# Attention scores from 64x32 tiles, value products from 64x64 and 32x64 tiles, in a fused attention and mixing kernel

## The chip, the cores and the metric

One NeuronCore of a Trainium2 chip. The metric is device microseconds (us) of one execution. The names of engines: PE is TensorE (matmul), PEld its weight loads, DVE VectorE, ACT ScalarE, POOL GpSimd, SP the engine whose queue issues nearly all DMA transfers. "Stationary" is the operand of a matmul that is loaded into the array, "moving" the one that streams through it. A tile "RxC" is a part of PE's array with R rows (the contraction) and C columns (the stationary operand's columns, which become output partitions).

## The reference

Eight batches, eight heads, 576 positions, 64 columns a head. Two parts: attention in a narrow window, then a mixing block on its result.

```python
B, H, S, D = q.shape                      # 8, 8, 576, 64
scores = (1 / sqrt(D)) * q @ k^T
rel = pos[:, None] - pos[None, :]
mask_plain = (rel >= 0) & (rel < 32)                       # heads 0 to 3
mask_dil = (rel >= 0) & (rel < 128) & (rel % 4 == 0)       # heads 4 to 7
attn = softmax(where(mask, scores, -1e9))
x = concat_heads(attn @ v)                # [B, 576, 512]

theta = x @ w_theta                       # 512 x 512
zr, zi = x * cos(theta), x * sin(theta)
y = w_tok_r @ zr + w_tok_i @ zi           # over positions, 576 x 576
u = x + y
out = u + relu(u @ w_ch)
```

All is f32. The host reorders the positions of the dilated heads so that every fourth position stands together: then they too have a window of 32, inside four segments of 144.

## The kernel before

Heads go in pairs, four pairs a batch (heads 2p and 2p+1 are pair p; NP is 4). A pair's 576 queries are 18 blocks of 32 (QB), and a block sees 64 keys (BW): its own 32 and the 32 ahead of them.

- `scores` (matmuls at line 614): per block one f32 matmul with 128 rows (64 columns of one head over 64 of the other) and 64 columns: the query tile is block-diagonal, the host has put zeros where a head meets the other head's rows. Block 2n goes to output partitions 0 to 63 and block 2n+1 to 64 to 127, so 18 matmuls on two column tiles fill nine groups of 64 keys: five groups in one PSUM bank of tag `s`, four in the next. The second bank is claimed after the first's matmuls are issued.
- `mask_scores` (line 553, DVE): adds the mask, negates and takes the row's bound, one instruction for each of the nine groups. `exp` on ACT (line 649), row sums and reciprocal on DVE (652, 653), and on POOL the product with the reciprocal (line 655) give the probabilities `P`, 128 partitions x 576: quadrants of 32 partitions are (block parity e, head).
- `turn` (line 673, DVE): eight transposes, 32 partitions x 288 each, write P turned into `pt`, which holds per group and head 128 keys x 64 queries, block-diagonal, with zeros that POOL wrote once. Only batch 0 does this on PE: `flip` multiplies P by an identity into PSUM tiles `pT` (line 709), and DVE and ACT copy them into `pt` (684, 687).
- `pv` (line 773): per group and head one f32 matmul with 128 rows (keys of two blocks, one over the other), 64 value columns and 64 queries: 18 matmuls on two column tiles into `o`. Value tiles come as `va` (five groups) and `vb` (four). `x_evac` (line 733) copies `o` to `x` in SBUF, undoing the order of the dilated heads.

Then come `theta` (tile `th`, line 842), cosine and sine (DVE, ACT, POOL), the token mixing and the channel product (`c`, line 1477). For batches 0 and 1 the token mixing is direct (`y`, line 1444, eight units of 24 or so matmuls each), from batch 2 (FIRST) on it is a fast scheme that multiplies sums of blocks, in steps A, B, C and D (line 1235). These large products use operands split in two parts (names ending in h and l) and the whole array, 128 rows x 128 columns.

What sets the order. The class `Order` runs all these functions as generators. Each says which engine it wants next and for how many ns (`yield "PE", 1060`) or which event it waits for (`yield None, ("pt", b, pr)`), and `Order` lays the instructions of each engine out in one fixed sequence by rank and these numbers, before the program is built. On the chip each engine follows its sequence and waits on semaphores. For the start (batches 0 and 1) a table RANK sets ranks; from batch 1's token mixing on, `phase(b)` writes a plan: eight or more token steps of batch b, between them the scores and value products of batch b+1 (or b+2), then theta of b+1 and the channel units of b. Each entry has a due time from a cost in us.

Loads of q and k (`load_qk`) and of values are issued on SP's queue two pairs or so ahead. Batch 0 has its own tiles (`first_k`, `first_v`) and `mask_on_pe`, which adds the mask by a bf16 matmul.

Of the kernel before, what the change touches and what calls it, by code (L numbers as in the profile page):

```python
# [20 lines left out]
QB = 32  # L21
BW = 2 * QB
NJ = S // (2 * QB)
VA = 5
NC = DM // 128
# [187 lines left out]
SLACK = 500  # L213
LATENCY = dict(PE=100.0, DVE=100.0, ACT=130.0, POOL=130.0, DMA=1800.0)
# [35 lines left out]
def build(ctx, tc, qT, kT, vw, wth, wtk, wch, maskb, ident, identb, outT):  # L250
# [60 lines left out]
    def load_qk(n):  # L311
        if n >= B * NP:
            return
        b, pr = divmod(n, NP)
        yield "rank", due.get(("scores", b, pr), od.rank)
        r = yield from take("qk", 2)
        if od.steady and b > FIRST and pr < 2:
            yield None, ("vbi", b - 1, pr + 1)
        q = ap.tile([128, 2 * NJ, 2 * QB], F32, tag="q", name=f"q{b}_{pr}")
        k = ap.tile([128, S + 32], F32, tag="k", name=f"k{b}_{pr}")  # L320
        yield "DMA", dma(2 * S)
        pin(nc.sync.dma_start(q, qT[b, pr]))
        yield "DMA", dma(S + 32)
        pin(nc.sync.dma_start(k, kT[b, pr]))
        qks[b, pr] = (q, k, r)
        signal(("qk", b, pr))
# [51 lines left out]
    KE = S + 32  # L378
# [11 lines left out]
    mskb = cp.tile([128, 6, BW], BF16, name="mskb")  # L390
# [5 lines left out]
    def first_loads():  # L396
# [3 lines left out]
        for pr in range(NP):  # L400
# [4 lines left out]
            q = q.rearrange("p a b -> p (a b)").rearrange("p (a b) -> p a b", b=2 * QB)  # L405
            k = first_k[:, KE * pr:KE * pr + KE]
            yield "DMA", dma(2 * S)
# [19 lines left out]
    def consts():  # L427
# [4 lines left out]
        for n in range(2):  # L432
            t = cp.tile([128, NJ, 2, 2 * QB], F32, name=f"pt{n}")
            yield "POOL", 1040
            pin(nc.gpsimd.memset(t, 0.0))
            pts.append(t)
# [99 lines left out]
    def mask_of(pr, j):  # L536
        if j == 0:
            return 1
        return {2: 2, 4: 3, 6: 4, 7: 5}.get(j, 0) if pr >= NP // 2 else 0

    pmats, probs = {}, {}

    def strips():

        for hh in range(2):
            for e in range(2):
                for o in range(2):
                    yield hh, e, o
# [9 lines left out]

    def on_pe(b, pr):
        return b == 0  # L560
# [24 lines left out]
    def scores(b, pr):  # L585
        yield None, ("qk", b, pr)
        if b == 1 and on_pe(b, pr):
            yield None, "sin0"
# [11 lines left out]
        for g0, g1 in ((0, 5), (5, NJ)):  # L600
            ps, rel = yield from bank("s", f"s{b}_{pr}_{g0}")
            ps = ps[:, :(g1 - g0) * BW].rearrange("p (a b) -> p a b", b=BW)
            held[g0] = ps, rel
            if b == 2 and not od.steady:
                yield "LATER", SLACK
            masked = on_pe(b, pr)
            if masked:
                yield "PE", 150
                mask_on_pe(ps, pr, g0, g1)
            yield "PE", (148 if od.steady else 162) * (g1 - g0)  # L610
            for n in range(g0, g1):
                for e in range(2):
                    qb = 2 * n + e
                    pe(nc.tensor.matmul(ps[64 * e:64 * e + 64, n - g0], q[:, qb],  # L614
                                        k[:, QB * qb:QB * qb + BW], start=not masked, stop=not masked or n == g1 - 1))
            if masked:
                go(row_max(b, ps, rel, P, mx, g0, g1, ("mask", b, pr, g0)))
            else:
# [8 lines left out]
        if b and on_pe(b, pr):  # L627
            for g0, (ps, rel) in held.items():
                yield None, ("mask", b, pr, g0)
                yield "EXP", 335 * ps.shape[1]  # L630
                for n in range(ps.shape[1]):
                    table(nc.scalar.activation(P[:, g0 + n], ps[:, n], AF.Exp, bias=mx[:, g0 + n:g0 + n + 1],
                                               scale=SCALE, accum_out=sm[:, g0 + n, :1]))
                give(*rel)
        else:
            for g0 in (0, 5):
                yield None, ("mask", b, pr, g0)
# [5 lines left out]
        elif not on_pe(b, pr):  # L643
# [15 lines left out]
    def turn(b, pr):  # L659
# [4 lines left out]
        yield None, ("pv",) + divmod(b * NP + pr - 2, NP)  # L664
        P, rp = probs.pop((b, pr))
        pmats[b, pr] = pts[pr % 2]
        for i, (hh, e, o) in enumerate(strips()):
            if od.steady:
                yield "TURN" if i < 7 else "DVE", 482
            elif i % 2 == 0:  # L670
                yield "DVE", 940
            k0, p0 = QB * (2 * e + o), QB * (2 * e + hh)
            pin(nc.vector.transpose(pmats[b, pr][k0:k0 + QB, :, hh, QB * e:QB * e + QB],  # L673
                                    P[p0:p0 + QB, :, QB * o:QB * o + QB]))
        give("P", rp)
        signal(("pt", b, pr))

    def flip_evac(b, ps, rel, pr, g0, g1, key):
        for e in range(2):
            es, qs = slice(BW * e, BW * e + BW), slice(QB * e, QB * e + QB)  # L680
            n = (g1 - g0) * BW
            if e == 0:
                yield "DVE", dve(n)
                pin(nc.vector.tensor_copy(pmats[b, pr][es, g0:g1, :, qs], ps[es]))
            else:
                yield "ACT", act(n)
                pin(nc.scalar.copy(pmats[b, pr][es, g0:g1, :, qs], ps[es]))
        give(*rel)
        signal(key)

    def flip(b, pr):

        yield None, ("P", b, pr)
        if pr >= 1:
            yield None, ("fl", b, pr - 1)
        if b or pr >= 2:
            yield None, ("pv",) + divmod(b * NP + pr - 2, NP)
        yield None, "pts"
        pmats[b, pr] = pts[pr % 2]
        P, rp = probs.pop((b, pr))  # L700
        gs = (0, 5), (5, NJ)
        for i, (g0, g1) in enumerate(gs):
            ps, rel = yield from bank(FL0[i] if b == 0 else "xt"[i], f"pT{b}_{pr}_{g0}")
            ps = ps[:, :(g1 - g0) * BW].rearrange("p (a h b) -> p a h b", h=2, b=QB)
            yield "PE", 70 * (g1 - g0)
            for n in range(g0, g1):
                for e in range(2):
                    es = slice(BW * e, BW * e + BW)
                    pe(nc.tensor.matmul(ps[es, n - g0].rearrange("p a b -> p (a b)"), P[es, n], idt[es, es],
                                        start=True, stop=True))  # L710
            go(flip_evac(b, ps, rel, pr, g0, g1, ("fe", b, pr, g0)))
        signal(("fl", b, pr))
        for g0, _ in gs:
            yield None, ("fe", b, pr, g0)
        if b == 0:
            give(f"xh{pr}", 0)
        else:
            give("P", rp)
# [4 lines left out]
    def x_evac(b, pr, ps, rel, key):  # L723
        dst, src = xf[b, pr], ps
        if pr >= NP // 2:
            dst = dst.rearrange("p (j c) -> p c j", c=4)
            src = src.rearrange("p (c j) -> p c j", c=4)
# [29 lines left out]
    def pv(b, pr):  # L757
# [10 lines left out]
        ps = ps_v.tile([128, 2 * DM], F32, tag="v", name=f"o{b}_{pr}")[:, :S]  # L768
        yield "PE", 1060 if od.steady else 1300
        for j in range(NJ):  # L770
            v = va[:, j] if j < VA else vb[:, j - VA]
            for hh in range(2):
                pe(nc.tensor.matmul(ps[64 * hh:64 * hh + 64, BW * j:BW * j + BW], v[:, 64 * hh:64 * hh + 64],  # L773
                                    pmats[b, pr][:, j, hh], start=True, stop=True))
# [962 lines left out]
```

## Time and profile before

| | |
|---|---|
| median of 3 runs | 555.21 us (554.04 to 555.28) |
| profiled execution | 555.45 us, its span 553.7 us |
| PE busy | 528.7 us, 95% of the span, 5296 matmul rows |
| DVE busy | 435.5 us, 79% |
| ACT, POOL busy | 373.1 us (67%), 329.4 us (59%) |
| scores on PE | 1008 + 144 rows |
| value products on PE | 600 + 464 + 72 + 16 rows |
| transposes by `turn` on DVE | 224, 105.1 us |
| moved by DMA | 124.42 MB, mean 225 GB/s |

The span is what the trace covers; the time of an execution has some 1.7 us more around it. A row of the profile reads: line, engine, operation, output tile <- input tiles, shapes, count, then busy us and the mean ns of one, then the idle time of the engine ahead of these instructions and what ended most of it. PE's rows overlap (a matmul's row includes the time until its result is out), so how often one starts tells more than how long it lasts. The windows view gives for each stretch of the span the busy time of each engine, the granted PE clock, the DMA engines' busy share and GB/s. "PE A L1235 x18" in the chain is 18 matmuls of step A in a row on the chain.

### The profile page before, as it was taken

Reading aid. Unit: us, or ns where it says so; the run is one execution under the profiler, and the core shown is the slowest. Engines: PE = TensorE matmul, PEld = TensorE weight load, DVE = VectorE, ACT = ScalarE, POOL = GpSimd, SP = SyncE. Lnnn points to the kernel's source line nnn. Section 1 sums busy time; section 2 is a strip of 40 time slices with the busy share of each in tenths; the row PEclk is TensorE's granted clock in tenths of the full one; section 3 lists DMA queues with packets and bytes.
Section 4 is the critical chain, followed back from the end, with each engine's and each line's share of the span. In section 5 each row is a group of like instructions: output and inputs, shape, how many; then the busy total and the mean of one; then the engine's idle time right before and its main releaser. Section 6 shows DMA issues by size and latency. Waiting matters only on the chain.

```text
span 553.7 us, 14354 instructions
## 1 busy us (share of the span) xinstructions
PE 528.7 (95%) x5296; PEld 478.8 (86%) x5296; DVE 435.5 (79%) x1359; ACT 373.1 (67%) x1029; POOL 329.4 (59%) x347
## 2 busy tenths in 40 slices
PE   5798898999999999999999999999999999999997
PEld 4643887888899899989999899989999899989997
DVE  3878897995588797989799988989799978848322
ACT  1589977858928478768775786768776777467320
POOL 1327868899774175655468375646468365817660
PEclk9999799999999999999999999999999999999999
DMA  8985245633578938994599828993698727680722
GB/s 297 400 332 186 99 139 202 222 144 119 165 256 265 343 155 283 341 282 173 189 326 306 299 86 274 363 281 118 236 325 282 277 90 219 209 274 28 233 85 86
DMA packets 59127, 124.42 MB, mean 225 GB/s; under 512 B 5424, under 2 KB 24624, under 8 KB 58800
## 3 DMA queue, kind: packets, MB, share of 16 engines
q1 hardware_dynamic: 59056, 123.49, 65.1%
q8 instruction: 42, 0.69, 0.5%
q14 instruction: 29, 0.24, 0.1%
HBM read 99.88 MB, written 23.59 MB: 223 GB/s over the span
## 4 chain that ended last, share of the span: by engine, by line
PE 65%; DVE 10%; DMA 9%; ACT 7%; POOL 5%; issue 2%; SPq 1%; POOLq 0%; ACTq 0%; DVEq 0%
PE c L1477 15%; PE th L842 11%; PE C L1235 8%; PE A L1235 7%; PE D L1235 6%; PE o L773 5%; PE B L1235 4%; PE s L614 4%; DVE pt L673 4%; DMA va<-in_vw_dram 3%; PE y L1444 2%; PE th L824 2%; DMA xn<-xd 1%; DMA st_wtk<-in_wtk_dram 1%; DMA q<-in_qT_dram 1%
## 5 line engine op out<-in xcount | busy, mean ns | idle before, releaser
L673 DVE STREAM_TRANSPOSE pt<-P 32x288 f32<-32x288 f32 x224 | 105.1, 469 | 13.1 <-POOL P L655 8.8
L1477 PE MATMUL c<-u,late_wc 128*128 128x288 f32 x768 | 109.1, 296 | 1.2 <-DVE x L1453 1.0
L1477 PEld LDWEIGHTS c<-u,late_wc 128*128 128x128 f32 x768 | 105.5, 188 | 4.7 <-DVE x L1453 1.5
L649 ACT ACTIVATE P<-P,mx 128x64 f32<-128x64 f32 x252 | 84.4, 337 | 2.9 <-DVE mx L553 2.6
L842 PE MATMUL th<-wthh,xh 128*128 128x512 f32 x224 | 75.0, 395 | 0.2 <-DVE K L1377 0.2
L655 POOL TENSOR_TENSOR P<-P,mx 128x576 f32<-128x576 f32 x32 | 38.2, 1192 | 57.6 <-DVE mx L653 50.4
L553 DVE CUSTOM_DVE_ANT_0 P<-s,mskb 128x64 f32<-128x64 f32 x252 | 39.0, 218 | 18.0 <-PE s L614 17.7
L1251 ACT CAST u<-x 128x288 fp32r<-128x288 f32 x48 | 20.6, 430 | 45.3 <-DVE x L1261 44.8
L842 PEld LDWEIGHTS th<-wthh,xh 128*128 128x128 f32 x224 | 42.0, 188 | 9.6 <-DVE K L1377 0.4
L1253 POOL TENSOR_TENSOR u<-x,u 128x288 fp32r<-128x288 f32 x48 | 41.6, 872 | 14.4 <-ACT u L1251 14.0
L649 ACT ACTIVATION_READ_ACCUMULATOR P<-P,mx 128x1 f32 x252 | 47.3, 188 | 0.0
L842 PE MATMUL th<-wthl,xh 128*128 128x512 f32 x112 | 44.4, 396 | 0.0
L733 ACT COPY x<-o 128x576 f32<-128x576 f32 x32 | 29.4, 920 | 19.6 <-PE o L773 19.5
L489 POOL TENSOR_TENSOR zl<-g,zh 128x512 fp32r<-128x512 f32 x7 | 9.1, 1298 | 53.5 <-ACT zh L481 53.5
L614 PE MATMUL s<-k,q 128*64 128x64 f32 x1008 | 36.6, 225 | 2.7 <-DVE K L1377 2.2
L614 PEld LDWEIGHTS s<-k,q 128*64 128x64 f32 x1008 | 32.8, 139 | 7.1 <-issue 2.7
L1453 DVE SCALAR_TENSOR_TENSOR x<-c,x 128x288 f32<-128x288 f32 x64 | 28.4, 451 | 11.6 <-PE c L1477 11.4
L773 PEld LDWEIGHTS o<-pt,va 128*64 128x64 f32 x600 | 20.4, 137 | 11.7 <-DVE pt L673 3.2
L773 PE MATMUL o<-pt,va 128*64 128x64 f32 x600 | 24.8, 227 | 5.8 <-DVE pt L673 2.9
L1015 POOL TENSOR_TENSOR s<-f,x 128x256 f32<-128x256 f32 x24 | 17.8, 740 | 12.2 <-DVE f L1003 10.0
L842 PEld LDWEIGHTS th<-wthl,xh 128*128 128x128 f32 x112 | 21.0, 188 | 4.2
L1095 POOL TENSOR_TENSOR s1l<-s,s1h 128x512 fp32r<-128x512 f32 x12 | 15.4, 1288 | 14.0 <-ACT s1h L1092 14.0
(232 smaller groups left out, 1576.3 us busy)
## 6 DMA issues: line engine op xcount, KB each, us to landing
q<-in_qT_dram SPq DMA_DIRECT2D x32, 576.0 KB, 6.0
late_wt_a<-tw_t SPq DMA_DIRECT2D x24, 576.0 KB, 6.8
wt_g<-tw_b SPq DMA_DIRECT2D x22, 576.0 KB, 6.4
va<-in_vw_dram SPq DMA_DIRECT2D x30, 320.0 KB, 4.9
k<-in_kT_dram SPq DMA_DIRECT2D x28, 304.0 KB, 6.2
out_dram<-x SPq DMA_DIRECT2D x28, 288.0 KB, 2.1
vb<-in_vw_dram SPq DMA_DIRECT2D x29, 256.0 KB, 4.5
xd<-xq SPq DMA_DIRECT2D x24, 288.0 KB, 5.3
```

Of the source, the lines that this page charges most:

```text
L553: pin(nc.vector.tensor_tensor_reduce(out=P[:, n], in0=ps[:, n - g0], in1=mskb[:, mask_of(pr, n)], op0=ALU.add, op1=ALU.min, scale=-SCALE, ...
L614: pe(nc.tensor.matmul(ps[64 * e:64 * e + 64, n - g0], q[:, qb], k[:, QB * qb:QB * qb + BW], start=not masked, stop=not masked or n == g1 - 1))
L649: table(nc.scalar.activation(P[:, n], P[:, n], AF.Exp, bias=mx[:, n:n + 1], scale=-1.0, accum_out=sm[:, n, :1]))
L655: pin(nc.gpsimd.tensor_tensor(P, P, mx.unsqueeze(2).to_broadcast([128, NJ, BW]), op=ALU.mult))
L673: pin(nc.vector.transpose(pmats[b, pr][k0:k0 + QB, :, hh, QB * e:QB * e + QB], P[p0:p0 + QB, :, QB * o:QB * o + QB]))
L733: pin(nc.scalar.copy(dst, src))
L773: pe(nc.tensor.matmul(ps[64 * hh:64 * hh + 64, BW * j:BW * j + BW], v[:, 64 * hh:64 * hh + 64], pmats[b, pr][:, j, hh], start=True, stop=T ...
L842: pe(nc.tensor.matmul(pt, l, r, start=(n == 0), stop=(n == 3 * NC - 1)))
L1235: pe(nc.tensor.matmul(ps, l, r, start=first and n == 1, stop=last and n == 3 * len(ks), skip_group_check=more))
L1253: pin(nc.gpsimd.tensor_tensor(ul[b, d][:, ts], x[:, ts], uh[b, d][:, ts].bitcast(F32), op=ALU.subtract))
L1453: pin(nc.vector.scalar_tensor_tensor(out=x[:, ts], in0=ps, scalar=0.0, in1=x[:, ts], op0=ALU.max, op1=ALU.add))
L1477: pe(nc.tensor.matmul(ps, l[:, cs], r[:, ts], start=(n == 0), stop=(n == 3 * NC - 1)))
```

## The change

- Scores: the queries have no zeros any more. A block of one head is its own matmul: 64 rows (that head's columns) x 32 stationary columns (its queries), 64 moving keys. 36 f32 matmuls a pair, on eight tiles: two row halves (the heads) by four column quadrants. Blocks are paired as n and n+9. To make eight tiles meet, the host swaps the heads' row halves for the groups of the second bank, and the matmuls of a group of the first bank and one of the second alternate, four and four. So for batch 1 on both `s` banks are claimed ahead of the first matmul, and the masks of both banks follow the last one.
- q loses its zeros (576 KB to 288 KB a pair), k has 704 columns in place of 608 (304 KB to 352 KB).
- `turn`: for "wide" pairs (pairs 0 and 2 of batches 2 to 7) eight 32x288 transposes as before, into another layout; for all others (all of batches 0 and 1, pairs 1 and 3 of the rest) one 128x576 transpose, which turns each 32x32 block where it lies.
- `pv`: `pt` has no zeros any more and no block-diagonal form. Wide: 36 matmuls on four 64x64 tiles, 64 keys x 64 value columns, 32 moving queries. Narrow: the keys of a block lie in two quadrants' worth of separate 32-row pieces, so 72 matmuls on 32x64 tiles, 32 moving queries, two of them accumulating to one result; four tiles are used.
- `flip` and its copies go, and batch 0 uses `turn`; POOL's two memsets of `pt` go; masks have five columns for six.
- New numbers for the planner: scores 660 ns, wide 600, narrow 1100 (before 148 per group, that is 1332, and 1060), phase costs .7, .7 and 1.2 us (before 1.35).

```diff
+SC_NS, PV_NS, PW_NS = 660, 1100, 600
+WIDE = (0, 2)
+def wide(b, pr):
+    return b >= FIRST and pr in WIDE
...
-        q = ap.tile([128, 2 * NJ, 2 * QB], F32, tag="q", name=f"q{b}_{pr}")
-        k = ap.tile([128, S + 32], F32, tag="k", name=f"k{b}_{pr}")
+        q = ap.tile([128, 2 * NJ, QB], F32, tag="q", name=f"q{b}_{pr}")
+        k = ap.tile([128, KE], F32, tag="k", name=f"k{b}_{pr}")
...
 def scores(b, pr):
-        for g0, g1 in ((0, 5), (5, NJ)):
+        def block(n, e):
+            qb = n + NJ * e
+            ko = QB * (qb + 1 + 2 * e + (n >= JS)) - QB
+            for r in range(2):
+                rs, to = slice(64 * r, 64 * r + 64), QB * (2 * e + (r if n < JS else 1 - r))
+                ps = held[0 if n < JS else JS][0]
+                pe(nc.tensor.matmul(ps[to:to + QB, n % JS], q[rs, qb], k[rs, ko:ko + BW],
+                                    start=b > 0, stop=b > 0 or n in (JS - 1, NJ - 1)))
+        for g0, g1 in groups:
             ps, rel = yield from bank("s", f"s{b}_{pr}_{g0}")
...
-            yield "PE", (148 if od.steady else 162) * (g1 - g0)
-            for n in range(g0, g1):
-                for e in range(2):
-                    qb = 2 * n + e
-                    pe(nc.tensor.matmul(ps[64 * e:64 * e + 64, n - g0], q[:, qb],
-                                        k[:, QB * qb:QB * qb + BW], start=not masked, stop=not masked or n == g1 - 1))
+        if b:
+            yield "PE", SC_NS
+            for i in range(JS):
+                for g0, g1 in groups:
+                    if g0 + i < g1:
+                        for e in range(2):
+                            block(g0 + i, e)
+            for g0, g1 in groups:
+                ps, rel = held[g0]
                 go(mask_scores(ps, rel, P, mx, pr, g0, g1, ("mask", b, pr, g0)))
...
 def turn(b, pr):
-        for i, (hh, e, o) in enumerate(strips()):
+        if wide(b, pr):
+            pw = pmats[b, pr].rearrange("p (n h) s -> p n h s", h=2)
+            for i in range(8):
+                e, o, hh = i // 4, i // 2 % 2, i % 2
+                k0, p0 = QB * (2 * e + o), QB * (2 * e + hh)
+                pin(nc.vector.transpose(pw[k0:k0 + QB, :, hh], P[p0:p0 + QB, :, QB * o:QB * o + QB]))
+        else:
+            yield "DVE", 790
+            pin(nc.vector.transpose(pmats[b, pr], P.rearrange("p n (o s) -> p (n o) s", s=QB)))
...
 def pv(b, pr):
-            for hh in range(2):
-                pe(nc.tensor.matmul(ps[64 * hh:64 * hh + 64, BW * j:BW * j + BW], v[:, 64 * hh:64 * hh + 64],
-                                    pmats[b, pr][:, j, hh], start=True, stop=True))
+            if wide(b, pr):
+                for e in range(2):
+                    for hh in range(2):
+                        rs = slice(64 * e, 64 * e + 64)
+                        pe(nc.tensor.matmul(ps[64 * hh:64 * hh + 64, e, QB * j:QB * j + QB], v[rs, 64 * hh:64 * hh + 64],
+                                            pmats[b, pr][rs, 2 * j + hh], start=True, stop=True))
+                continue
+            for o in range(2):
+                for e in range(2):
+                    for hh in range(2):
+                        rs = slice(QB * (2 * e + hh), QB * (2 * e + hh) + QB)
+                        pe(nc.tensor.matmul(ps[64 * hh:64 * hh + 64, e, QB * j:QB * j + QB], v[rs, 64 * o:64 * o + 64],
+                                            pmats[b, pr][rs, 2 * j + o], start=(o == 0), stop=(o == 1)))
...
-        go(flip(0, p), RANK["flip"][p])
+        go(turn(0, p), RANK["flip"][p])
```

Three places in the fixed order. A row names the line, the operation, output tile <- inputs (tile numbers behind a name count tiles), the moving part's form and how many stand in a row. First PE in a steady phase, before: the value product of pair 3 and the next batch's scores of pair 1, one after the other.

```order
L773 MATMUL o_3_4972<-pt_118,va_3_4756 64x64 x10
L773 MATMUL o_3_4972<-pt_118,vb_3_4836 64x64 x8
L614 MATMUL s_1_0_4997<-k_1_4759,q_1_4758 64x64 x10
L614 MATMUL s_1_5_5018<-k_1_4759,q_1_4758 64x64 x8
```

The same place after the change:

```order
L745 MATMUL o_3_5083<-pt_117,va_3_4832 64x32 x40
L745 MATMUL o_3_5083<-pt_117,vb_3_4935 64x32 x32
L601 MATMUL s_1_0_5168<-k_1_4835,q_1_4834 32x64 x4
L601 MATMUL s_1_5_5169<-k_1_4835,q_1_4834 32x64 x4
L601 MATMUL s_1_0_5168<-k_1_4835,q_1_4834 32x64 x4
L601 MATMUL s_1_5_5169<-k_1_4835,q_1_4834 32x64 x4
```

The two groups stand next to each other as before; the product has 72 matmuls for 18, and the scores alternate between their two banks, four matmuls at a time.

DVE in a steady phase, before, where pairs 0 and 1 are turned between other work of the token steps:

```order
L673 STREAM_TRANSPOSE pt_116<-P_0_4832 32x9x32
L1261 TENSOR_TENSOR x_0_3698<-D_0_4931,x_0_3698 128x288
L673 STREAM_TRANSPOSE pt_116<-P_0_4832 32x9x32 x2
L1261 TENSOR_TENSOR x_1_3829<-D_1_4941,x_1_3829 128x288
L673 STREAM_TRANSPOSE pt_116<-P_0_4832 32x9x32
L673 STREAM_TRANSPOSE pt_118<-P_1_4995 32x9x32 x4
```

And after:

```order
L1231 TENSOR_TENSOR x_3_5082<-C_1_6095,x_3_5082 128x288
L673 STREAM_TRANSPOSE pt_116<-P_0_6037 32x9x32 x4
L651 TENSOR_REDUCE mx_1_6274<-sums_97 128x9
L652 RECIPROCAL mx_1_6274<-mx_1_6274 128x9
L1231 TENSOR_TENSOR x_0_4592<-D_0_6147,x_0_4592 128x288
L673 STREAM_TRANSPOSE pt_116<-P_0_6037 32x9x32 x2
L1231 TENSOR_TENSOR x_1_4756<-D_1_6159,x_1_4756 128x288
L676 STREAM_TRANSPOSE pt_117<-P_1_6273 128x576
```

Pair 0 keeps its eight pieces, pair 1 has one instruction.

PE at batch 0's token mixing (units y), before, where the first value product of batch 1 stands:

```order
L614 MATMUL s_2_5_922<-k_2_698,q_2_697 64x64 x8
L1444 MATMUL y_3_0_928<-wt_g,z_1_674 128x288 x3
L773 MATMUL o_0_900<-pt_116,va_0_435 64x64 x10
L773 MATMUL o_0_900<-pt_116,vb_0_436 64x64 x8
L1444 MATMUL y_3_0_928<-wtkh_544,z_4_571 128x288
```

And after:

```order
L601 MATMUL s_2_0_1030<-k_2_888,q_2_887 32x64 x4
L1414 MATMUL y_0_0_965<-wt_g,z_0_770 128x288 x3
L745 MATMUL o_0_1027<-pt_116,va_0_589 64x32 x40
L745 MATMUL o_0_1027<-pt_116,vb_0_590 64x32 x32
L1414 MATMUL y_0_0_965<-wt_g,z_3_964 128x288 x3
```

The product has moved from the fourth unit (y_3) into the first (y_0), behind the scores of pair 2 in both.

More of the change, by code (lines that the diff above doesn't have):

```diff
@@ L24 @@
 VA = 5
+JS = 5
+KE = 32 * (2 * NJ + 4)
 NC = DM // 128
@@ L389, in build @@
     idt = ids[:, :128]
-    mskb = cp.tile([128, 6, BW], BF16, name="mskb")
+    mskb = cp.tile([128, 5, BW], BF16, name="mskb")
     idb = ids[:, 128:192].bitcast(BF16)
@@ L432, in consts @@
         for n in range(2):
[L433 to L436, printed above, removed]
+            pts.append(cp.tile([128, 2 * NJ, QB], F32, name=f"pt{n}"))
         signal("pts")
@@ L536, in mask_of @@
     def mask_of(pr, j):
-        if j == 0:
-            return 1
-        return {2: 2, 4: 3, 6: 4, 7: 5}.get(j, 0) if pr >= NP // 2 else 0
+        if pr < NP // 2:
+            return int(j == 0)
+        return {0: 2, 4: 3, 5: 4}.get(j, 0)
     pmats, probs = {}, {}
-    def strips():
-        for hh in range(2):
-            for e in range(2):
-                for o in range(2):
-                    yield hh, e, o
     def mask_scores(ps, rel, P, mx, pr, g0, g1, key):
@@ L626, in scores @@
             go(load_qk(b * NP + pr + 2), RANK["load"][0])
[L627 to L637, printed above, removed]
+        for g0 in (0, JS):
+            yield None, ("mask", b, pr, g0)
         if b == 0:
@@ L663, in turn @@
         yield None, ("P", b, pr)
-        yield None, ("pv",) + divmod(b * NP + pr - 2, NP)
+        if b or pr >= 2:
+            yield None, ("pv",) + divmod(b * NP + pr - 2, NP)
         P, rp = probs.pop((b, pr))
         pmats[b, pr] = pts[pr % 2]
-        for i, (hh, e, o) in enumerate(strips()):
-            if od.steady:
-                yield "TURN" if i < 7 else "DVE", 482
[L670 to L715, printed above, removed]
+        if wide(b, pr):
[3 more added lines that the diff above has]
+                k0, p0 = QB * (2 * e + o), QB * (2 * e + hh)
+                yield "TURN" if i < 7 else "DVE", 482
+                pin(nc.vector.transpose(pw[k0:k0 + QB, :, hh], P[p0:p0 + QB, :, QB * o:QB * o + QB]))
+        else:
+            yield "DVE", 790
+            pin(nc.vector.transpose(pmats[b, pr], P.rearrange("p n (o s) -> p (n o) s", s=QB)))
@@ L716, in flip @@
+        if b:
+            give("P", rp)
+        else:
             give(f"xh{pr}", 0)
-        else:
-            give("P", rp)
         signal(("pt", b, pr))
@@ L767, in pv @@
         n = yield from take("v", 1)
-        ps = ps_v.tile([128, 2 * DM], F32, tag="v", name=f"o{b}_{pr}")[:, :S]
-        yield "PE", 1060 if od.steady else 1300
+        ps = ps_v.tile([128, 2 * DM], F32, tag="v", name=f"o{b}_{pr}").rearrange("p (e c) -> p e c", e=2)
+        yield "PE", PW_NS if wide(b, pr) else PV_NS
         for j in range(NJ):
             v = va[:, j] if j < VA else vb[:, j - VA]
-            for hh in range(2):
-                pe(nc.tensor.matmul(ps[64 * hh:64 * hh + 64, BW * j:BW * j + BW], v[:, 64 * hh:64 * hh + 64],
-                                    pmats[b, pr][:, j, hh], start=True, stop=True))
+            if wide(b, pr):
[6 more added lines that the diff above has]
+            for o in range(2):
+                for e in range(2):
+                    for hh in range(2):
+                        rs = slice(QB * (2 * e + hh), QB * (2 * e + hh) + QB)
+                        pe(nc.tensor.matmul(ps[64 * hh:64 * hh + 64, e, QB * j:QB * j + QB], v[rs, 64 * o:64 * o + 64],
+                                            pmats[b, pr][rs, 2 * j + o], start=(o == 0), stop=(o == 1)))
         go(x_evac(b, pr, ps, ("v", n), ("xe", b, pr)))
@@ L1511, in phase @@
                     if pv_at[p] == n:
-                        yield ("pv", nb, p), pv(nb, p), 1.35
+                        yield ("pv", nb, p), pv(nb, p), .7 if wide(nb, p) else 1.2
         rest = UNITS[8:]
@@ L1570, in steady @@
             prev = key
-            if key[0] == "sc" and not on_pe(*key[1:]):
+            if key[0] == "sc":
                 go(turn(*key[1:]), t)
```

87 lines of the change are left out of this document (46 added, 41 removed).

## The prediction

> **What bounds the kernel now.** I read the page first (busy shares, the chain that ended last), then windows of stages, then the rows of PE (TensorE) in one steady stretch.
>
> ```profile
> span 553.7 us, 14354 instructions
> PE 528.7 (95%) x5296; PEld 478.8 (86%) x5296; DVE 435.5 (79%) x1359; ACT 373.1 (67%) x1029; POOL 329.4 (59%) x347
> PE 65%; DVE 10%; DMA 9%; ACT 7%; POOL 5%; issue 2%; SPq 1%; POOLq 0%; ACTq 0%; DVEq 0%
> ...
> core 0: us, PE busy (x) PEld busy (x) DVE busy (x) ACT busy (x) POOL busy (x), PEclk, DMA share, GB/s
> 0.00:33.00 33.00, 23.63 (x464) 18.17 (x464) 20.14 (x52) 12.59 (x22) 7.12 (x10) 1.00 0.95 355
> 33.00:60.00 27.00, 22.51 (x126) 10.12 (x124) 23.50 (x62) 26.32 (x44) 18.23 (x14) 0.94 0.58 205
> 60.00:104.00 44.00, 40.07 (x428) 37.22 (x428) 37.95 (x127) 35.28 (x124) 34.56 (x31) 0.96 0.51 172
> 104.00:166.00 62.00, 59.36 (x599) 53.51 (x599) 46.28 (x151) 43.15 (x122) 52.85 (x59) 1.00 0.51 170
> 207.00:268.40 61.40, 61.40 (x640) 57.49 (x634) 55.08 (x184) 45.98 (x135) 37.36 (x41) 1.00 0.76 257
> ...
> 207.19 2.58 PE A L1235 x18
> 268.60 2.58 PE A L1235 x18
> 330.01 2.58 PE A L1235 x18
> 391.43 2.58 PE A L1235 x18
> ```
>
> Three limits, one after the other. Until 33 us the DMA engines are 95% busy. From 33 to 60 us ACT is busy 26.3 of 27 us. From there on it is PE: the chain meets the same step A every 61.4 us, and in 207 to 268 PE is busy all of 61.40 us, so there an instruction more or less on PE is worth its own time and no wait is there to be won. DVE (55.1 of 61.4) is second. I count six such phases, the one from 104 us (with 2.6 us of idle PE) and five full ones. In each PE does four score groups and four value products; the last stretch, from 476 us, has none of them.
>
> **What one group costs on PE now.** An f32 matmul shows as two rows, so 18 matmuls are x36.
>
> ```profile
> L614 PE MATMUL s<-k,q 128*64 128x64 f32 x1008 | 36.6, 225 | 2.7 <-DVE K L1377 2.2
> L773 PE MATMUL o<-pt,vb 128*64 128x64 f32 x464 | 19.0, 223 | 0.3 <-DMA vb<-in_vw_dram 0.2
> ...
> 344.11 0.29 PE L1235 MATMUL A<-late_wt_a,s2l 128*128 128x288 f32 x1
> 344.34 0.80 PE L773 MATMUL o<-pt,va 128*64 128x64 f32 x20
> 344.97 0.64 PE L773 MATMUL o<-pt,vb 128*64 128x64 f32 x16
> 345.44 1.22 PE L614 MATMUL s<-k,q 128*64 128x64 f32 x36
> 346.59 0.54 PE L1235 MATMUL C<-wt_g,s3h 128*128 128x288 f32 x2
> 346.96 0.29 PE L1235 MATMUL C<-wt_g,s3l 128*128 128x288 f32 x1
> ```
>
> Only starts are used here, since rows overlap. The 16 rows from 344.97 end at the start of the next group at 345.44: .47 us, 29.4 ns a row. Two tiles (64 columns each) take turns, so one tile starts a row every 58.8 ns, and a group of 36 rows is 1.06 us. From 344.11 to 346.96 are 2.85 us; less three steps of the 288-wide product (2.58/18, less the tail, .133 each) and less 2 x 1.06, .33 us is left for going from the whole array to small tiles and back. Eight groups: 8.48 us a phase.
>
> **What a row of a small tile is made of: weights or stream.** This decides the forecast.
>
> ```profile
> L824 PEld LDWEIGHTS th<-st_wth,x 128*128 128x128 f32 x32 | 5.3, 188 | 5.6 <-issue 3.1 <-DMA st_wtk<-in_wtk_dram 0.9 <-DVE st_wtk L465 0.9
> L824 PEld LDWEIGHTS th<-st_wth,x 128*64 128x64 f32 x8 | 0.8, 134 | 2.5 <-issue 2.4
> 26.65 0.30 PEld L824 LDWEIGHTS th<-st_wth,x 128*128 128x128 f32 x2
> 28.47 0.19 PEld L824 LDWEIGHTS th<-st_wth,x 128*64 128x64 f32 x2
> ```
>
> Two loads back to back span .30 us with 128 columns, where one has 188 ns: the second began .11 us after the first. With 64 columns it is .19 less .134, .056 us. So an f32 load occupies its tile for about .055 us per 64 columns, which is just what the tile's present pitch is; the present stream of 64 moving columns is at most 58.8 ns too. The trace can't part the two today, since both operands have 64 columns. After the change they differ: scores have 32 stationary and 64 moving columns, value products 64 stationary and 32 moving. I take the load as exposed where it is the longer one.
>
> **The change, part by part.**
>
> Scores: 36 matmuls, 72 rows on eight tiles, 9 rows each. Load .028, stream .0588, so 9 x .0588 = .53 us for 1.06. Bounds: .53 (eight at once) and 1.06 (no more overlap than now). I take .53, because two tiles of different rows already run at once in the trace:
>
> ```profile
> 22.71 1.26 PE L709 MATMUL pT<-ids,P 64*64 64x64 f32 x36 [0.48 <-POOL P L655]
> ```
>
> These 36 rows are 64x64 tiles on the diagonal, two row halves writing one bank, and take 1.26 us with the last row's tail of .22: the same pitch. A rule speaks against eight at once: the Trainium skill, "TensorEngine Tiling (Array Packing)", section "Gotcha 1: PSUM Pressure", says that different row tiles cannot access the same PSUM bank at the same time, and here one head's tiles of group n and the other's write one bank. By it scores would stay at 1.06 and a phase would be 2.12 us longer than in my sum; the row of pT differs from it, as far as two diagonal tiles show.
>
> Value products, wide (two pairs a phase): 36 matmuls, 72 rows on four tiles, 18 each. By the load 18 x .055 = .99; by the stream of 32 columns (half of .0588) .54. Narrow (two pairs): 72 matmuls, 144 rows, 36 a tile: 1.98 or 1.08. I take .99 and 1.98, by the load rows above, and keep .54 and 1.08 for the range.
>
> Switching between two small shapes: PE goes from value tiles (64 wide) to score tiles (32 wide) without the whole array in between.
>
> ```profile
> 15.67 0.68 PE L709 MATMUL pT<-ids,P 64*64 64x64 f32 x16
> 16.28 0.80 PE L614 MATMUL s<-first_k,q 128*64 128x64 f32 x20
> ```
>
> 16 rows at 29.4 ns are .47 of these .61 us: .14 us for the switch. Three of a phase's five excursions hold a pair: +.42 us. Bounds 0 and .33 each (a full excursion).
>
> Sum of a phase on PE: 4 x .53 + 2 x .99 + 2 x 1.98 + .42 = 8.48, against 8.48. Net 0.0, by six phases 0; what scores win, the narrow products give back.
>
> DVE's turning: eight 32x288 transposes become one 128x576 for narrow pairs.
>
> ```profile
> L673 DVE STREAM_TRANSPOSE pt<-P 32x288 f32<-32x288 f32 x224 | 105.1, 469 | 13.1 <-POOL P L655 8.8
> L897 DVE STREAM_TRANSPOSE xq<-x 128x576 f32<-128x576 f32 x24 | 17.7, 762 | 1.0 <-ACT x L733 0.9
> 93.44 0.74 PE L773 MATMUL o<-pt,va 128*64 128x64 f32 x17 [1.72 <-DVE pt L673]
> 104.42 0.74 PE L773 MATMUL o<-pt,va 128*64 128x64 f32 x17 [1.17 <-DVE pt L673]
> ```
>
> 8 x .469 - .76 = 3.0 us less on DVE per narrow pair. In the steady phases (6 us of 55) that lies beside a full PE and is worth nothing. In batch 1 it takes away the two waits, 2.9 us; there four score groups save 2.12 and four narrow products add 4 x .92 = 3.68. Together -1.3. Bounds -4 (narrow by the stream, waits gone) and +3 (the waits go to something else, next in line is POOL's multiply of P).
>
> Batch 0: the 72 rows of pT a pair and their copies go (four pairs), narrow products add 3.68, and POOL's two memsets of pt go. All this lies in the first 33 us, under DMA; the cover is the 95% row. What counts there is bytes.
>
> ```profile
> q<-in_qT_dram SPq DMA_DIRECT2D x32, 576.0 KB, 6.0
> k<-in_kT_dram SPq DMA_DIRECT2D x28, 304.0 KB, 6.2
> ```
>
> q halves to 288 KB, k grows to 352: 240 KB a pair, .98 MB for the four pairs of batch 0, at 355 GB/s 2.8 us. I take -2.8; bounds -4 (later pairs' loads move up too) and 0 (the stage ends on another transfer). In later phases the DMA share is .76 and the saving is hidden.
>
> Both score banks are now claimed before the first matmul, and the masks start after the second bank's. What this can hold up stands here:
>
> ```profile
> 330.90 0.08 DVE L553 DVE_READ_ACCUMULATOR2_ANT mx<- 128x1 f32 x1
> 333.62 1.22 PE L614 MATMUL s<-k,q 128*64 128x64 f32 x36
> ```
>
> The masks of the pair ahead are done at 330.98, 2.6 us ahead of the next group, so the wait costs nothing. If the masks came 2.6 us later, PE's whole queue would stand behind that group.
>
> Total: 555.45 (profiled execution; its span is 553.7, and the median of the runs is 555.21, .24 lower, which I leave out) - 2.8 - 1.3 + 0 = **551.3 us**. Its own range is 546 to 557: the bounds of start (+2.8), batch 1 (-2.7, +4.3), and .4 us a phase if a load-bound row keeps 58.8 ns in place of 55. About 0.3% (1.7 us) is what a measurement tells from no change.
>
> **Rivals.**
>
> A, the load isn't exposed: the next weights come in while two or more tiles stream, and value products run at .54 and 1.08. A phase is 2.12 + 1.08 + 2.16 + .42 = 5.78, 2.70 less; 16.2 us in six, and some 1.8 in batch 1: **533**. For it: PE now hides loads fully behind streams of 64. Against: the .056 us of the 64-column load, measured with nothing else on PE.
>
> B, the other side: scores get no more overlap, through the shared bank or because both row halves' tiles take their moving columns in turn. A group stays at 1.06, +2.12 a phase and in batch 1: 551.3 + 7 x 2.12 = **566**. It decides from about .68 us a group on: 28 groups x .15 eat the 4.1 us that my sum wins. Against it stands the pT row; for it, that no row has more than two tiles at once.
>
> C, the change doesn't do what it says: two rows of one f32 matmul stand next to each other on PE and only two tiles ever run. Scores 2.12, wide 1.98, narrow 3.96, +12.3 a phase: **625**. Two tiles do overlap now with the same issue of rows, so little speaks for it.
>
> D, a new wait in batch 1. The first value product of batch 1 now stands inside the first token unit; before, it stood after three.
>
> ```profile
> 60.16 1.06 PE L1444 MATMUL y<-wt_g,z 128*128 128x288 f32 x3 [1.12 <-DVE mx L553]
> 63.84 0.96 PE L1444 MATMUL y<-wt_g,z 128*128 128x288 f32 x6
> 66.04 1.18 POOL L655 TENSOR_TENSOR P<-P,mx 128x576 f32<-128x576 f32 x1 [0.69 <-DVE mx L653]
> ```
>
> The first unit runs from 60.16 to 63.84; P is ready at 67.2 and turned at 68.0. If exponentials and POOL don't come earlier, PE stands some 4.4 us with all token units queued behind: 551.3 + 4.4 = **555.7**. Against it: DVE is freed ahead of that, and q and k come 2.8 us earlier.
>
> **How the numbers follow.** Chances: my case .43, A .28, B .16, D .09, C .04. The point is my case's 551.3. From 530 to 567 lie my case, D, nearly all of A and most of B; left out are C, the upper third of B and the edge of A, near .12. Faster by over 0.3% (under 553.5): .34 of my case, A, .02 of D: .64. Within 0.3%: .08 and .05: .13. Slower: B, C, and .03 of the others: .23.
>
> **What would show it.** The start-to-start time of a score group of 72 rows: .53 us right, 1.06 is B. A wide product of 72 rows: .99 right, .54 is A; a narrow one of 144: 1.98 or 1.08. The step A of the chain every 61.4 us, or 58.7 (A), 63.5 (B). PE idle ahead of the first product of batch 1 is D. The first DMA-bound stretch should end near 30 us. I am wrong if loads overlap within a tile, if eight tiles don't run, or if the start ends on something else than bytes.

## The result and the profile after

The change made the kernel slower: 611.61 us median (608.30 to 613.95, four runs) against 555.25 us before; ratio 1.1012, 95% interval 1.0943 to 1.1081. The profiled execution took 609.35 us, its span 607.6. The forecast was 551.3, a little faster than before, with a range to 567; the kernel got much slower.

Page lines after, and of before the one that was not shown yet (q8, a queue that brings instructions: packets, MB, share of the DMA engines' time):

```profile
span 607.6 us, 21409 instructions
PE 557.6 (92%) x8888; PEld 503.9 (83%) x8888; DVE 386.6 (64%) x1243; ACT 370.7 (61%) x1021; POOL 326.0 (54%) x345
q8 instruction: 70, 1.15, 0.8%
PE 84%; issue 5%; DVE 4%; ACT 4%; DMA 2%; POOL 1%; SPq 0%; POOLq 0%; DVEq 0%
```

```profile
q8 instruction: 42, 0.69, 0.5%
```

PE has 3592 more matmul rows and as many more loads, DVE 49 us less work, and the chain has 5% "issue", time in which PE waited for nothing that the profile shows. The windows from the start to the first step A of a steady phase, from there to the sixth, and the rest; first before, then after:

```profile
0.00:207.19 207.19, 185.94 (x1957) 156.27 (x1957) 162.59 (x488) 145.52 (x385) 131.65 (x136) 0.98 0.63 221
207.19:511.83 304.64, 304.24 (x3054) 284.49 (x3055) 260.30 (x843) 219.33 (x628) 179.46 (x193) 1.00 0.71 239
511.83:553.70 41.87, 38.47 (x289) 38.00 (x287) 12.65 (x30) 8.24 (x17) 18.27 (x19) 1.00 0.40 135
```

```profile
0.00:234.53 234.53, 202.33 (x3497) 170.25 (x3497) 144.42 (x436) 143.35 (x378) 131.64 (x135) 0.88 0.55 180
234.53:565.68 331.15, 316.82 (x5106) 295.67 (x5107) 229.80 (x779) 219.27 (x628) 176.43 (x193) 0.98 0.65 209
565.68:607.60 41.92, 38.48 (x288) 38.01 (x287) 12.35 (x29) 8.12 (x17) 17.97 (x19) 1.00 0.39 133
```

Of the 53.9 us the start lost 27.3, the five phases 26.5, the tail nothing. In the phases PE was idle .4 us before and is 14.3 us now; the other 12.6 are busy time. In the start PE's idle time grew by 11 us and its busy time by 16, at a granted clock of .88 for .98. What PE waited for, after:

```profile
PE o L745 <- issue: 15.3, 7, 3.7
PE s L601 <- issue: 9.5, 5, 3.8
...
PE C L1205 <- issue: 1.8, 1, 1.8
...
PE A L1205 <- issue: 0.6, 1, 0.6
```

27.2 us, nearly all inside a group, where the next matmul of the same loop waits for no other engine. Before it was 1.3:

```profile
PE pT L709 <- issue: 0.8, 1, 0.8
...
PE s L614 <- issue: 0.5, 1, 0.5
```

Two pieces of PE's timeline after:

```profile
244.40 1.37 PE L745 MATMUL o<-pt,va 32*64 32x32 f32 x80
245.59 1.11 PE L745 MATMUL o<-pt,vb 32*64 32x32 f32 x64
246.63 0.54 PE L1205 MATMUL A<-late_wt_a,s2h 128*128 128x288 f32 x2
...
316.43 0.78 PE L738 MATMUL o<-pt,va 64*64 64x32 f32 x40
317.03 0.65 PE L738 MATMUL o<-pt,vb 64*64 64x32 f32 x32
317.61 0.78 PE L601 MATMUL s<-k,q 64*32 64x64 f32 x55
321.12 0.35 PE L601 MATMUL s<-k,q 64*32 64x64 f32 x17 [2.74 <-issue]
```

A narrow product is 2.23 us to the next group's start (244.40 to 246.63) and a wide one 1.18 (316.43 to 317.61); from their first row to their last, read from the single rows, 2.08 and 1.03. The score group that follows runs 55 of its 72 rows, stands for 2.74 us and runs the other 17. Undisturbed groups show what scores cost without that:

```profile
160.86 0.97 PE L601 MATMUL s<-k,q 64*32 64x64 f32 x72
161.76 0.53 PE L1414 MATMUL y<-wt_g,z 128*128 128x288 f32 x2
```

.90 us to the next work (1.15 to 1.20 before), .76 from first row to last.

### The profile page after: what moved, and what is told of

It reads as the page before. It is cut to its first block, busy times and chain, and to the rows that moved or that the text cites. A ratio compares the mean times of both kernels' runs of the same rounds, so it can differ in the third digit from the quotient of the medians.

```text
span 607.6 us, 21409 instructions
## 1 busy us (share of the span) xinstructions
PE 557.6 (92%) x8888; PEld 503.9 (83%) x8888; DVE 386.6 (64%) x1243; ACT 370.7 (61%) x1021; POOL 326.0 (54%) x345
## 3 DMA queue, kind: packets, MB, share of 16 engines
q8 instruction: 70, 1.15, 0.8%
## 4 chain that ended last, share of the span: by engine, by line
PE 84%; issue 5%; DVE 4%; ACT 4%; DMA 2%; POOL 1%; SPq 0%; POOLq 0%; DVEq 0%
PE c L1447 16%; PE th L812 12%; PE o L745 9%; PE C L1205 9%; PE y L1414 8%; PE A L1205 7%; PE D L1205 7%; PE s L601 5%; PE B L1205 4%; PE o L738 2%; PE th L794 2%; PE th L817 1%; PE th L816 1%; DMA st_wch<-in_wch_dram 1%; ACT P L648 1%
## 5 line engine op out<-in xcount | busy, mean ns | idle before, releaser
L648 ACT ACTIVATE P<-P,mx 128x64 f32<-128x64 f32 x252 | 84.4, 337 | 12.6 <-DVE mx L551 12.6
L1223 POOL TENSOR_TENSOR u<-x,u 128x288 fp32r<-128x288 f32 x48 | 39.8, 840 | 23.9 <-ACT u L1221 23.9
L673 DVE STREAM_TRANSPOSE pt<-P 32x288 f32<-32x288 f32 x96 | 45.0, 469 | 3.3 <-POOL P L654 1.3
L601 PE MATMUL s<-k,q 64*32 64x64 f32 x2016 | 30.1, 235 | 12.0 <-issue 9.5
L601 PEld LDWEIGHTS s<-k,q 64*32 64x32 f32 x2016 | 23.9, 111 | 16.9 <-issue 13.0
L745 PEld LDWEIGHTS o<-pt,va 32*64 32x64 f32 x1440 | 24.7, 142 | 6.6 <-ACT st_wth L467 2.9
L745 PE MATMUL o<-pt,va 32*64 32x32 f32 x1440 | 26.7, 227 | 2.9 <-issue 2.8
L745 PE MATMUL o<-pt,vb 32*64 32x32 f32 x1088 | 21.7, 227 | 7.5 <-issue 7.5
L745 PEld LDWEIGHTS o<-pt,vb 32*64 32x64 f32 x1088 | 19.9, 144 | 7.9 <-issue 7.9
L494 POOL TENSOR_TENSOR u<-x,u 128x288 fp32r<-128x288 f32 x15 | 14.4, 961 | 20.1 <-ACT u L486 12.9
```

What stands on the lines that cost most here:

```text
L601: pe(nc.tensor.matmul(ps[to:to + QB, n % JS], q[rs, qb], k[rs, ko:ko + BW], start=b > 0, stop=b > 0 or n in (JS - 1, NJ - 1)))
L648: table(nc.scalar.activation(P[:, n], P[:, n], AF.Exp, bias=mx[:, n:n + 1], scale=-1.0, accum_out=sm[:, n, :1]))
L673: pin(nc.vector.transpose(pw[k0:k0 + QB, :, hh], P[p0:p0 + QB, :, QB * o:QB * o + QB]))
L745: pe(nc.tensor.matmul(ps[64 * hh:64 * hh + 64, e, QB * j:QB * j + QB], v[rs, 64 * o:64 * o + 64], pmats[b, pr][rs, 2 * j + o], start=(o == ...
L1223: pin(nc.gpsimd.tensor_tensor(ul[b, d][:, ts], x[:, ts], uh[b, d][:, ts].bitcast(F32), op=ALU.subtract))
```

## The experiments

In the edits below "..." stands for code that is left out.

Theory 1: in dense groups PE runs out of instructions, and the stands lower its clock behind them; the groups' own time is the smaller part. The rival: the weight loads of the products are the loss, and the waits have another cause.

**Every pair wide.**

```diff
 def wide(b, pr):
-    return b >= FIRST and pr in WIDE
+    return True
```

> The change, with every pair wide (64x64 tiles, eight transposes) where 20 of 32 pairs were narrow. In the profile after, a wide product is 1.03 us from first to last row and a narrow one 2.08, and PE stands 27 us for 'issue' in and behind the small-tile groups. Theory 1 (PE runs out of instructions in dense groups, and its clock drops after such stands): 20 x 1.05 us of product go, 1440 of the 8888 matmul rows go, and the issue waits fall with them from 27 to some 12 us; about 575 us. Rival (the weight loads of the products are all that is lost, the waits have another cause): 21 us less and the issue waits stay, about 590 us. DVE gets 60 us more and stays below PE.

582.40 us, ratio to before 1.0486 (1.0427 to 1.0545): 29 us less than the change, 21 by the products' own time. PE's rows are 7448, and its issue waits fell to 4.4 us, more than expected. The time alone decides nothing: it is 7 us above theory 1's number and 8 below the rival's. The waits speak for theory 1; the rival expected them to stay. In the start PE waits for DVE now, whose eight transposes are back (9.2 of the 10.1 us):

```profile
PE o L738 <- DVE pt L673: 10.1, 15, 5.0
...
PE s L601 <- issue: 2.2, 2, 2.0
...
227.32:539.19 311.87, 305.96 (x4386) 282.92 (x4387) 258.72 (x843) 218.67 (x627) 178.84 (x193) 0.99 0.68 221
```

The five phases are 311.9 us, between before (304.6) and after (331.2).

**The scores alone**, on the kernel before (the new `scores`, q without zeros, k with 640 columns, blocks paired as before; products, turning and batch 0's `flip` untouched).

```diff
-                    pe(nc.tensor.matmul(ps[64 * e:64 * e + 64, n - g0], q[:, qb],
-                                        k[:, QB * qb:QB * qb + BW], ...))
+                    for r in range(2):
+                        pe(nc.tensor.matmul(ps[to:to + QB, n % JS], q[rs, qb], k[rs, ko:ko + BW], ...))
```

> The kernel before with the scores alone changed: 36 matmuls of 64x32 tiles, both banks together, q without zeros (288 KB), k 320 KB; transposes, products and batch 0's turning on PE as before. A score group should take .90 us to the next group where it took 1.15 to 1.20. Theory 1: 28 groups x .27 = -7.6 us and -2.8 us of DMA at the start, less some 5 to 10 us of new issue waits (1152 matmul rows more): 548 to 555 us. Rival (loads alone; scores cause no waits): 545 us, with the issue waits at 1 to 2 us as before.

562.68 us, ratio 1.0121 (1.0081 to 1.0161): slower by 1.2%, outside both forecasts. But not in the phases:

```profile
0.00:216.91 216.91, 185.80 (x2497) 155.50 (x2497) 167.35 (x486) 145.74 (x384) 130.30 (x135) 0.95 0.56 192
216.91:517.88 300.97, 300.97 (x3666) 280.24 (x3667) 260.39 (x847) 217.91 (x629) 179.25 (x197) 1.00 0.70 228
```

Five phases take 300.97 for 304.64 and PE is never idle in them: the score tiles win .73 us a phase. The start loses 9.7 us, with 6.1 us of issue waits, a wait of 5.2 us for DVE's g and a clock of .95 for .98; how much each of these costs was not parted. So half of the change was worth having in one place and not in the other.

**The products alone** (the change, with zeros in q and 18 matmuls for the scores).

```diff
-            for r in range(2):
-                pe(nc.tensor.matmul(ps[to:to + QB, n % JS], q[rs, qb], k[rs, ko:ko + BW], ...))
+            pe(nc.tensor.matmul(ps[64 * e:64 * e + 64, n % JS], q[:, qb], k[:, ko:ko + BW], ...))
```

> The change without its scores: queries keep their zeros (576 KB), 18 matmuls of 128x64 tiles a pair, one bank after the other; products wide and narrow and the turning as in the change. Theory 1: most of the loss stays, 590 to 600 us, with issue waits of 15 us or more in the narrow products. Rival (loads alone): 20 narrow products x 1.05 = +21 us less some waits for DVE, about 575 us, issue waits small.

609.64 us, ratio 1.0962 (1.0917 to 1.1007): as slow as the whole change, above even theory 1's range. 15.1 us of issue waits. The phases are 329.5 us. The old scores, whose groups were never broken by an issue wait before, now stand behind a narrow product:

```profile
328.78 1.11 PE L733 MATMUL o<-pt,vb 32*64 32x32 f32 x64
329.82 0.97 PE L599 MATMUL s<-k,q 128*64 128x64 f32 x25
333.44 0.57 PE L599 MATMUL s<-k,q 128*64 128x64 f32 x11 [2.64 <-issue]
```

A group of two-column tiles with the same 36 rows as in the kernel before stops after 25 of them. It isn't its own tiles; what changed is what ran ahead of it.

**Filler on the kernel before.** More PE instructions and no smaller tile: tiny bf16 matmuls on 128x64 tiles, two moving columns each.

```diff
                 pe(nc.tensor.matmul(ps[64 * hh:64 * hh + 64, BW * j:BW * j + BW], ...))
+                for f in range(6):
+                    hs = slice(64 * (f % 2), 64 * (f % 2) + 64)
+                    pe(nc.tensor.matmul(full[hs, S:S + 2], mskb[:, f % 6, :], mskb[:, 0, :2], start=True, stop=True))
```

> The kernel before with 108 tiny bf16 matmuls (64 columns, 2 moving columns, into unused columns of the product's banks) laid between the 18 matmuls of each value product: as many PE instructions as the change has, with no other tile shape and no narrow tiles; nothing of the result changes. Theory 1: PE stands for 'issue' 15 us or more in all, as in the change, though no product is narrow, and the clock drops with it. Rival (the waits come from the small tiles themselves): each product gets longer by the tiny matmuls (.6 to 1.2 us), and the issue waits stay at 1 to 3 us in all.

640.17 us (one run). The filler is dearer than reckoned, but the question was the waits: 18.4 us of issue, for 1.3 in the same kernel without filler, and 69 instruction packets for 42.

```profile
q8 instruction: 69, 1.13, 0.8%
...
PE s L614 <- issue: 7.2, 5, 2.4
PE o L778 <- issue: 6.9, 4, 2.4
...
PE s L568 <- issue: 3.0, 1, 3.0
...
476.61 0.22 PE L778 MATMUL o<-mskb 128*64 128x2 bf16 x3
479.20 0.22 PE L778 MATMUL o<-mskb 128*64 128x2 bf16 x3 [2.38 <-issue]
```

Without any of the change's tiles and with nothing but more instructions, PE stands for 1 to 3 us at a time, inside a loop of matmuls that wait for nobody. This tells the theories apart: the waits come from the number of instructions in a short time.

That the instructions come too late can be read from the trace, which holds the time of every packet of q8 (16384 bytes each). In the change all fourteen stands of over half a microsecond, which make up nearly all of the issue waits, end 1.3 to 1.6 us after such a packet has ended. Four of them:

| PE stands (us) | the packet before its end (us) | from the packet's end to PE's next row |
|---|---|---|
| 17.51 to 21.24 | 18.67 to 19.75 | 1.5 |
| 189.77 to 193.57 | 191.33 to 192.21 | 1.4 |
| 261.19 to 263.20 | 260.75 to 261.67 | 1.5 |
| 318.38 to 321.12 | 318.69 to 319.60 | 1.5 |

With 70 packets in 607.6 us a stand would end in such a stretch of .3 us by chance about once in thirty. All eleven stands of over half a microsecond with filler (1.2 to 1.6 us) and all ten with the products alone (1.2 to 1.6) do the same. One of four with every pair wide (.5 us) and one of three with the scores alone (2.3 us at 83.8) do not, and their cause stays open.

The count of packets fits too: the change has 28 more of them for 7184 more rows and loads of PE, the filler 27 for 6912, both times 64 bytes each. So q8 brings PE's instructions, 256 to a packet. A narrow product (144 rows and 144 loads in 2.08 us) uses up more than one packet; two groups of the kernel before, 36 rows and 36 loads in 1.06 us each, use little more than half of one in the same time. What decides when a packet is asked for, and how many are held ready, no run here shows.

**Load or stream.** The moving columns of the wide products doubled.

```diff
+                        w = 2 if j < NJ - 1 else 1
-                        pe(nc.tensor.matmul(ps[..., QB * j:QB * j + QB], v[...], pmats[b, pr][rs, 2 * j + hh], ...))
+                        pe(nc.tensor.matmul(ps[..., QB * j:QB * j + QB * w], v[...],
+                                            pmats[b, pr][rs, 2 * j + hh:2 * j + hh + w], ...))
```

> The change, with the moving operand of the wide products doubled: 64 columns a matmul in place of 32 (the second 32 are of no use, and the next group writes over their results, so the output stays the same). Theory 1 (a row of a product costs its 64-column weight load, .056 us, and the stream of 32 columns is hidden behind it): a wide product keeps its 1.03 us from first to last row. Rival (the stream sets the pace, and only two of four tiles run at once): about twice as long, 1.9 to 2.1 us.

```profile
237.83 0.81 PE L739 MATMUL o<-pt,va 64*64 64x64 f32 x40
238.46 0.62 PE L739 MATMUL o<-pt,vb 64*64 64x64 f32 x32
239.01 0.48 PE L601 MATMUL s<-k,q 64*32 64x64 f32 x33
```

237.83 to 239.01 is 1.18 us, as with 32 columns, and 1.03 from first row to last. Twice the stream costs nothing, so the stream of 32 columns did not set the pace. The load of 64 columns did, or a fixed price of a row; this run doesn't part the two. The four tiles do run at once: their rows start 6 to 7 ns apart, in rounds of 58.5 ns. The kernel took 607.90 us (one run), as the change does.

**Scores from batch 2 on**, on the kernel before: the old form for batches 0 and 1.

```diff
+            if b < FIRST:
...
+                        pe(nc.tensor.matmul(ps[64 * e:64 * e + 64, n - g0], q[:, qb],
+                                            k[:, QB * qb:QB * qb + BW], ...))
...
+        if b >= FIRST:
...
+            yield "PE", 900
```

> The kernel before with scores from 64x32 tiles in batches 2 to 7 only (24 of 32 pairs); batches 0 and 1 keep the zeros in q and their 18 matmuls. Theory 1 (what the scores-only kernel lost, it lost in its first 207 us, by new issue waits and the halved clock behind them; its steady phases were 60.67 us for 61.40): step A is first met at 207 us as before, phases stay at 60.67, no issue wait over .5 us in a score group; 551 to 552 us, ratio .992 to .995. Rival (the phases gained because the loss at the start had spread the transfers): no change, 555 us or more.

557.90 us, ratio 1.0020 (.9992 to 1.0047): no change, the rival's number, though not for its reason. The five phases kept their gain, 301.7 us for 304.6; two of them took 60.65 us each:

```profile
210.53 2.57 PE A L1265 x18
272.07 2.57 PE A L1265 x18
332.72 2.57 PE A L1265 x18
393.37 2.57 PE A L1265 x18
...
PE o L803 <- DVE pt L703: 3.6, 1, 3.6
```

The first step A came 3.3 us late. Batch 2's first two score groups are placed in the start by the planner; with their new form and costs the order around them changed, and one value product at 96 us waits 3.6 us for its transposes, where two products waited 2.9 us before. A gain of 3.0 us in the phases was given back in the start, where PE stood idle 2.6 us longer in all and the clock was .96 for .98; no single wait made the loss.

**The lone four first**, on the same kernel.

```diff
-            for i in range(JS):
+            for i in (4, 0, 1, 2, 3):
```

> As the late-scores kernel, with the four matmuls that have no partner in the second bank put first in each score group in place of last. A score group of 72 rows took .76 us from first to last where 9 rows a tile x .056 would be .50; its first 40 rows come 7 ns apart, then there is a gap and the rest come 8.3 ns apart. If the lone four (half the tiles) make the loss, it moves to the front and the group keeps or cuts its length by up to .05; if the gap stays at row 40, it is a limit on how fast PE is handed matmuls, and the group keeps .76.

556.17 us (one run); 22 of the 24 groups still take .76 us from first row to last, the other two .78 and .81. In the change's undisturbed groups the first 32 rows start within .24 us, mostly 6 to 7 ns apart; then comes a gap of some .09 us, and from there it is 16 to 17 ns a matmul. So the .76 is not the half-used last round. That the second part is a limit on how fast f32 matmuls are handed on (some 16.7 ns each) fits, but was not tried by itself.

**Scores from batch 3 on**, all in the steady phases, so that the start is the old one (the edit is against the kernel of batch 2 on).

```diff
+NEW = 3
-            if b < FIRST:
+            if b < NEW:
```

> As the late-scores kernel, with scores from 64x32 tiles only in batches 3 to 7 (20 of 32 pairs), all of them in the steady phases; the start is that of the kernel before (the late-scores kernel got a wait of 3.6 us for DVE's transposes at 96 us, where its two pairs of batch 2 had changed the order). Theory 1: step A first at 207 us, five phases of 60.65 for 61.4, so 3.5 us less than before: ratio .992 to .996. Rival (the phases' gain is lost in the tail or in the first phase): ratio 1.

551.69 us, ratio .9908 (.9881 to .9935): faster than both kernels, by 4.8 us (.9%) of the median beside it.

```profile
PE 524.9 (95%) x6016; PEld 473.9 (86%) x6016; DVE 435.0 (79%) x1359; ACT 371.0 (67%) x1029; POOL 326.7 (59%) x347
...
207.02 2.78 PE A L1266 x18
267.88 2.57 PE A L1266 x18
328.53 2.57 PE A L1266 x18
...
507.79 2.39 PE A L1266 x18
```

The first step A is where it was (207), and the sixth comes at 507.79 for 511.83. The five phases give 3.9 us of it.

## Why the prediction was wrong

**The step that failed** is "Net 0.0, by six phases 0", and behind it the sentence that an instruction more or less on PE is worth its own time. The sum counted durations and not instructions. 3592 more rows and their loads made PE stand 27.2 us, and the case of PE running out of instructions was in none of the rivals. The trace of before had its hint: the row of the instruction queue (42 packets of 16 KB) and 1.3 us of issue. The stand of .80 us in that trace, too, ends 1.4 us after a packet of that queue. The filler shows this cause without any of the change's tiles, and the times of the packets show it in the change itself.

**What follows a stand** was not in the sum either: the clock. One stand at 189 us, with windows of the same kernel around it:

```profile
189.33 0.44 PE L601 MATMUL s<-k,q 64*32 64x64 f32 x28
193.57 0.68 PE L601 MATMUL s<-k,q 64*32 64x64 f32 x32 [3.80 <-issue]
...
185.00:189.80 4.80, 4.77 (x189) 4.40 (x187) 1.04 (x2) 3.99 (x20) 2.39 (x3) 1.00 0.84 216
193.60:200.00 6.40, 6.40 (x67) 6.23 (x68) 2.84 (x22) 3.09 (x18) 2.40 (x2) 0.51 0.52 159
200.00:207.00 7.00, 7.00 (x55) 7.00 (x54) 5.64 (x14) 1.23 (x2) 2.37 (x3) 1.00 0.36 71
...
322.72:326.13 3.41, 3.41 (x17) 3.41 (x16) 1.28 (x6) 3.31 (x16) 1.30 (x2) 0.50 0.49 149
```

The granted clock is 1.00 ahead of it, .51 for 6.4 us behind it, and 1.00 again: 3.8 us of standing cost about 3.1 more. The Trainium skill, "TensorE: Matmul & The Clock Gate", Part 1, says that the clock falls to half after an idle window of about 3.4 us. The stand of 3.80 agrees, but shorter ones cost something too: in the five phases the clock was at half for three stretches of 3.41 us, which began .3 to 1.6 us behind the stands of 2.74 (the last row above), 2.00 and 2.38 us. Behind those of 1.40, 1.75, 1.80 and .65 it stayed at 1.00, while with the products alone a stand of 1.40 us was followed by such a stretch; the runs give no length from which on it happens. In the start the first stand was 3.73 us long, from 17.5 us on, with two more of 1.26 and 2.83 us up to 33; the clock was at .50 from 18.9 to 42.8 us, where before it was 1.00 from 12.6 to 56.9.

**Weights or stream: right in size.** Wide .99 forecast, 1.03 measured; narrow 1.98 forecast, 2.08 measured; the doubled stream shows that the 32 moving columns don't set the price. That the load does rests on the .056 us of one 64-column load in the trace of before. A fixed price of some 58 ns a row would give the same, and no run has both operands under 64 columns. Rival A, that loads are hidden, is refuted, and so is C (two tiles only).

**Scores: half right.** .53 forecast, .76 measured; 1.06 would have been B. Eight tiles do run at once for the first 32 rows, two row halves into one bank: these rows start within .24 us. The Trainium skill, "TensorEngine Tiling (Array Packing)", "Gotcha 1: PSUM Pressure", says that different row tiles can't access the same PSUM bank at the same time; it did not hold the pace at 1.06 here. The term was mis-sized by .23 us a group, .9 a phase.

**Switches: right.** The pair's second lead is .15 us (.14 forecast).

With these sizes, groups and switches make a phase 1.3 us longer, from first row to the next group's start (4 x .90 + 2 x 1.18 + 2 x 2.23 = 10.42 us for 9.15, the eight groups before at 1.10 to 1.20). The prediction gave each of the five phases four score groups; the last one has only one, and loses 1.9. Together that is 7.0 us. The phases lost 26.5: 13.9 are idle time (12.7 us of issue waits make up most of it, one wait of 1.5 us for a load comes next), and 7.0 are the groups. Of the other 5.6 the three stretches at half clock (10.2 us) can explain up to 5.1. The step A that the prediction named as its sign came after 66.2 to 68.8 us in four phases, for 61.4 to 61.8 before, and after 60.8 in the last, for 58.6; the last has one stand, of .65 us.

Two sums of the prediction are off without weight for this: its named bounds add up to 547 to 561, not 546 to 557, and by its own rows rival D's stand is 4.1 us (63.84 to 67.98), not 4.4.

**The start: wrong in sign.** -2.8 and -1.3 were forecast, +27.3 came. Fewer bytes did not end the first stretch earlier: PE stood in its products there, and the transfers ran at a mean 180 GB/s up to the first step A, for 221 before. That loads waited for tiles which late products still held is argued from this, not shown. Of the 16 us more of busy time up to step A the clock can explain about all: it was at half for 47.8 us more than before, and PE was busy for 33.7 of them, so up to 17 us. The narrow products' share in it was not measured by itself. "All this lies in the first 33 us, under DMA" holds only while PE stays ahead of DMA; the cover was gone.

**Rival D** did not come about as told; the first product of batch 1 waited for no P. The waits for DVE's transposes (2.9 us) went, as forecast; the issue waits of the start, 14.6 us, are many times that.

## What to carry to other kernels

Count a change's instructions per microsecond beside its durations. Where a group of matmuls is cut into smaller tiles, each matmul keeps its load and its place in the instruction stream, and an engine that is 100% busy at 34 rows a microsecond may stand at 70 once such groups follow one another. Then count the rows that each tile gets: in these runs a tile of any of the small shapes started a row every 56 to 59 ns, with 32 or 64 stationary and 32 or 64 moving columns, as long as nothing else held it up. The scores went from 18 rows a tile to 9 and gained, though less than half; the wide products stayed at 18 and gained nothing; the narrow ones went to 36 and lost. In this kernel the score tiles paid where they stood among large products, in the steady phases, and cost time in the start.

## What the runs showed of the hardware

Not expected, with their numbers: PE stands of 1 to 4 us in the middle of a loop once dense groups follow one another (27.2 us in the change, 18.4 with filler; 1.0 and 1.2 in the two kernels with score tiles only from batch 2 or 3 on, as before with 1.3), and behind nearly every one of over half a microsecond it goes on 1.2 to 1.6 us after the end of a packet of 256 instructions. A tile starts an f32 row every 58 to 59 ns with 64 stationary columns, whether it has 128, 64 or 32 rows and 64 or 32 moving columns (18, 18 and 36 rows a tile in 1.05, 1.03 and 2.08 us). Eight 64x32 tiles start 6 to 7 ns apart for 32 rows and then slow to about 16.7 ns a matmul. Half clock came in stretches of 3.41 us or multiples of it, also behind stands of 2.0 to 2.7 us.
